# A fused attention and MLP block on one core: reordered weight loads, a spread reciprocal root, a new order in the first block and a split tail

## The chip, the cores and the metric

The kernel runs on one core of a Trainium2 chip. The metric is the device time of one execution in microseconds (us). The span that a profile shows, from the first to the last instruction of the program, is about 2 us shorter (708.9 us where the device time is 710.91). Repeated executions are compared by their median, and ratios are of means.

## The reference, cut to what matters

```python
x = A_x                                             # (1, 2048, 1024), bf16
h  = x + attention(layernorm(x)) @ wo               # 32 heads of 32, window of 256 tokens
h2 = h + silu(layernorm(h) @ w1) @ w2               # w1: 1024 x 3584, w2: 3584 x 1024
```

Tokens are handled in four blocks of 512. The stages follow each other: Q, K and V of block 0; then, for b = 1 to 3, attention of block b-1 woven with the projections of block b; then attention of block 3 woven with the output projections (wo) of blocks 0 to 2; then the MLP of each block. The output projections of block 3 are woven into the first MLP stage.

## The kernel before: the parts that the argument touches

All DMAs are issued from one queue, in program order, on the sync engine (SP in the profile). Attention output is transposed by DMA. The issue of a transpose is deferred to the next step with a list:

```python
late = []
def run_late():
    while late:
        late.pop(0)()
...
def end():                                   # last part of one head group
    attn_out(b, g, 11, 16)
    late.append(lambda: attn_transpose(b, g))
```

The first MLP stage finishes the last head group in its first three iterations (`extra`), then loads four of the seven 1 MB pieces of w2. From iteration 6 on it weaves in the output projections of block 3, which read that last transpose:

```python
run_late()
load_w2(5)
for ft in range(FT):
    acc = h1_group(b, ft)
    run_late()
    if extra:
        extra.pop(0)[0]()
        if not extra and b == 0:
            for i in (1, 2, 3, 4):
                load_w2(i)
    silu(b, acc, ft)
    if b == 0 and 6 <= ft < 14:
        wo_group(NB - 1, *divmod(ft - 6, 2))     # needs every head group's transpose
```

In the attention stages there are only two accumulator banks, and VectorE empties one of them after each group of eight matmuls. VectorE also does the layer normalisation of a coming block, with the reciprocal root by three Newton steps, all in one lump:

```python
def ln_rstd(st, rs, lo, hi):                 # twelve instructions on [128, 4]
    ...
    for _ in range(3):
        nc.vector.scalar_tensor_tensor(out=ta, in0=y, scalar=-0.5, in1=va, ...)
        nc.vector.tensor_tensor(out=ta, in0=ta, in1=y, op=ALU.mult)
        nc.vector.scalar_tensor_tensor(out=y, in0=ta, scalar=1.5, in1=y, ...)
```

The softmax here doesn't subtract the row's maximum and nothing guards it: scores larger than these inputs give would overflow.

## Time and profile before

| | before |
|---|---|
| median of 4 executions, us | 709.91 (707.37 to 710.03) |
| span of the profiled execution, us | 708.9 (device time 710.91, longer than all four above) |
| TensorE busy | 695.2 us, 98% |
| TensorE waits that the profile names | 10.4 us in six entries |

The prediction below shows the main views. In a timeline line, the first two numbers are the start and the length in us, and square brackets give the idle time before it and what ended that. In a window line, the length is followed by the busy time of TensorE, its weight loads, VectorE, ScalarE and GpSimd, then by the granted clock (the share of full speed that TensorE was allowed), the DMA share and GB/s. Two more views help. The first is the page's list of DMA issues (what is written and read, how many, KB each, median us from issue to landing): a transpose of attention output usually lands in 2.5 us, a piece of w2 in 9.0.

```profile
r_a<-in_B_w_dram SPq DMA_DIRECT2D x7, 1024.0 KB, 9.0
...
r_a<-r_n SPq DMA_TRANSPOSE x32, 2.5
```

The second is the page's row of TensorE's granted clock over 40 slices of 17.7 us, in tenths of full speed (9 is 90% or more). One slice, from about 301 to 319 us, shows an 8.

```profile
PEclk9999999999999999989999999999999999999999
```

### The profile page before, as it was taken

To read this page: it belongs to the slowest core of one execution; us is meant where nothing else is said; L and a number is where in the kernel's file an instruction comes from. 1 tells how busy PE (TensorE), PEld (TensorE's weight loads), DVE (VectorE), ACT (ScalarE), POOL (GpSimd) and SP (SyncE) were. 2 spreads that over 40 slices of the span, in tenths; PEclk is the share of its full clock that TensorE was granted. 3 is DMA by queue.
4 is the path that set the end of the run, shared out by engine and by line. 5 is a ranking of instruction groups with operands and counts; after the bars stand their busy time and mean duration, and the time that the engine had idled before them with its cause. 6 is when DMAs were issued, how large, how long until landed. Compare 5 with 4: busy or idle time off the path is not lost.

```text
span 708.9 us, 12138 instructions
## 1 busy us (share of the span) xinstructions
PE 695.2 (98%) x5006; PEld 332.8 (47%) x5006; DVE 288.0 (41%) x606; ACT 259.7 (37%) x335; POOL 172.9 (24%) x375
## 2 busy tenths in 40 slices
PE   8999999999999999979999999999999999999998
PEld 3444555555555554534444444444444444444443
DVE  5347645834443448523332423325134352243111
ACT  3416667777777777511220013300033200233000
POOL 1006566777777777500000000000000000000000
PEclk9999999999999999989999999999999999999999
DMA  9540322125011899780122320021410032200110
GB/s 301 173 120 8 46 54 75 32 55 180 16 23 18 279 265 333 201 276 31 45 69 90 80 75 1 0 67 59 78 35 0 1 97 67 75 1 0 31 38 22
DMA packets 75127, 60.55 MB, mean 85 GB/s; under 512 B 48960, under 2 KB 59200, under 8 KB 75072
## 3 DMA queue, kind: packets, MB, share of 16 engines
q1 hardware_dynamic: 75072, 59.78, 29.9%
q8 instruction: 39, 0.64, 0.4%
q14 instruction: 16, 0.13, 0.1%
HBM read 39.85 MB, written 8.39 MB: 68 GB/s over the span
## 4 chain that ended last, share of the span: by engine, by line
PE 94%; DMA 4%; DVE 2%; SPq 0%; issue 0%
PE hacc L446 18%; PE hacc L483 17%; PE acc L220 16%; PE acc L483 10%; PE acc L446 9%; PE acc L212 8%; PE acc L239 5%; PE o_ps L293 5%; PE sc L257 4%; DMA r_a<-r_n 2%; DMA r_w<-in_A_wqkv_dram 1%; PE hacc L239 1%; DMA r_a<-in_A_x_dram 1%; DVE ln_st L157 0%; DVE r_t L241 0%
## 5 line engine op out<-in xcount | busy, mean ns | idle before, releaser
L268 ACT ACTIVATE r_e<-sc 128x1024 bf16<-128x1024 f32 (+2 forms) x192 | 175.8, 967 | 67.5 <-PE sc L257 54.5
L283 POOL TENSOR_SCALAR_AFFINE_SELECT r_e<-r_e 128x256 bf16<-128x256 bf16 (+1 forms) x368 | 169.9, 490 | 123.1 <-ACT r_e L268 119.7
L446 PEld LDWEIGHTS <-r_w 128*128 128x128 bf16 x896 | 87.8, 98 | 106.1 <-issue 2.4
L483 PEld LDWEIGHTS <-r_a 128*128 128x128 bf16 x896 | 87.7, 98 | 105.7
L483 PE MATMUL hacc<-r_a 128*128 128x512 bf16 x560 | 122.3, 379 | 0.0
L446 PE MATMUL hacc<-r_e,r_w 128*128 128x512 bf16 x456 | 100.9, 379 | 0.0
L455 ACT ACTIVATE r_n<-hacc 128x512 f32<-128x512 f32 x30 | 17.9, 597 | 178.9 <-PE hacc L446 178.9
L483 PE MATMUL acc<-r_a 128*128 128x512 bf16 x336 | 74.0, 379 | 0.0
L220 PEld LDWEIGHTS <-r_w 128*128 128x128 bf16 x512 | 46.1, 98 | 58.6 <-issue 8.9
L222 DVE CAST r_a<-acc 128x512 bf16<-128x512 f32 x56 | 38.6, 690 | 81.0 <-PE acc L220 55.8
L293 PEld LDWEIGHTS <-r_e 128*128 128x128 bf16 x1440 | 50.3, 96 | 22.7
L220 PE MATMUL acc<-r_t,r_w 128*128 128x512 bf16 x256 | 60.8, 380 | 0.0
L220 PE MATMUL acc<-r_w 128*128 128x512 bf16 x256 | 58.2, 380 | 0.0
L293 PE MATMUL o_ps<-r_a,r_e 128*128 128x33 bf16 x1440 | 51.2, 178 | 0.0
L239 PE MATMUL acc<-r_o,r_a 128*128 128x512 bf16 x208 | 49.4, 380 | 1.3 <-DVE r_t L241 1.3
L446 PE MATMUL acc<-r_e,r_w 128*128 128x512 bf16 x216 | 49.1, 379 | 0.0
L239 PEld LDWEIGHTS <-r_a 128*128 128x128 bf16 x256 | 23.3, 98 | 37.2 <-issue 7.4
L257 PE MATMUL sc<-r_a 32*128 32x128 bf16 (+2 forms) x704 | 37.2, 276 | 0.0
L496 DVE SCALAR_TENSOR_TENSOR r_t<-hacc,r_t 128x512 bf16<-128x512 f32 x20 | 13.7, 683 | 56.3 <-PE hacc L483 56.2
L446 PE MATMUL hacc<-r_a,r_w 128*128 128x512 bf16 x144 | 34.6, 393 | 0.0
L496 DVE SCALAR_TENSOR_TENSOR r_t<-acc,r_t 128x512 bf16<-128x512 f32 x12 | 8.3, 692 | 64.2 <-PE acc L483 64.2
L456 DVE SCALAR_TENSOR_TENSOR r_a<-r_n,hacc 128x512 bf16<-128x512 f32 x30 | 20.6, 688 | 33.1 <-ACT r_n L455 33.1
(65 smaller groups left out, 425.4 us busy)
## 6 DMA issues: line engine op xcount, KB each, us to landing
r_w<-in_B_w_dram SPq DMA_DIRECT2D x8, 896.0 KB, 6.8
r_a<-in_B_w_dram SPq DMA_DIRECT2D x7, 1024.0 KB, 9.0
r_w<-in_A_wqkv_dram SPq DMA_DIRECT2D x5, 1024.0 KB, 11.8
r_o<-in_A_x_dram SPq DMA_DIRECT2D x16, 256.0 KB, 5.0
h_dram<-r_t SPq DMA_DIRECT2D x16, 256.0 KB, 2.9
r_t<-h_dram SPq DMA_DIRECT2D x16, 256.0 KB, 2.8
out_dram<-r_t SPq DMA_DIRECT2D x32, 128.0 KB, 1.7
r_e<-h_dram SPq DMA_DIRECT2D x3, 1024.0 KB, 5.8
```

The lines of the kernel that those rows point to most:

```text
L212: nc.tensor.matmul(acc, lhsT=lnT_b[b % 2][:, kt, j * P:(j + 1) * P], rhs=wqkv[:, kt, col0:col0 + 512], start=(kt == 0), stop=(kt == KT - 1))
L220: nc.tensor.matmul(acc, lhsT=wqkv[:, kt, col0:col0 + P], rhs=lnT_b[b % 2][:, kt, :], start=(kt == 0), stop=(kt == KT - 1))
L222: copy(out=(qT, kT)[which][b][:, g, :], in_=acc)
L239: nc.tensor.matmul(acc, lhsT=qT[b][:, g, j * P:(j + 1) * P], rhs=wo[:, g, c * 512:(c + 1) * 512], start=(g == 0), stop=(g == G - 1))
L257: nc.tensor.matmul(sc[hh // 2][:, hh % 2, ch * P:(ch + nq) * P], lhsT=kT[t // 4][r0:r0 + DH, g, (t % 4) * P:(t % 4 + 1) * P], rhs=qT[b][r0 ...
L268: nc.scalar.activation(out=e[:, :, lo:hi], in_=sc[pair][:, :, lo:hi], func=ACT.Exp, scale=scale)
L283: nc.gpsimd.affine_select(out=ap, in_=ap, pattern=[[0, 2], [0, n], [sgn, P]], compare_op=ALU.is_ge if upper else ALU.is_gt, fill=0.0, base ...
L293: nc.tensor.matmul(o_ps[pair][:, qt * 2 + hh, 0:VW], lhsT=e_of(i, kind, pair)[:, hh, ch * P:(ch + 1) * P], rhs=v[:, b * 4 + kt, g * 4 + pa ...
L446: nc.tensor.matmul(acc, lhsT=w1[:, kt, ft * P:(ft + 1) * P], rhs=ln2T[b][:, kt, :], start=(kt == 0), stop=(kt == KT - 1))
L456: nc.vector.scalar_tensor_tensor(out=gT[:, ft, :], in0=th, scalar=1.0, in1=acc, op0=ALU.add, op1=ALU.mult)
L483: nc.tensor.matmul(acc, lhsT=gT[:, ft, j * P:(j + 1) * P], rhs=w2[ft // 4][:, ft % 4, c * 512:(c + 1) * 512], start=(ft == 0), stop=(ft == ...
L496: nc.vector.scalar_tensor_tensor(out=t_out[j % 2][:, c * 512:(c + 1) * 512], in0=acc, scalar=0.5, in1=t_in[j % 2][:, c * 512:(c + 1) * 512 ...
```

## The change

Its intent: take away what TensorE waits for. Separate V weights leave the region of three w1 chunks free earlier; block 0 loads x tiles and weights and orders its V groups in another way, with three warm-up matmuls fewer (matmuls on zeros ahead of the first real work, whose results nobody uses); the Newton steps are spread; four w2 loads come later; the last output columns are split so that the last eviction and store are short. The core of the diff, with cuts marked:

```diff
-    wqkv = view(r_w, 0, KT, 3 * D)
+    wqk = view(r_w, 0, KT, 2 * D)
+    wv = view(r_w, 16384, KT, D)
@@ first loads
     load_x(0, 0)
-    load_wqkv(2 * D, 0, 4)
     load_x(0, 1)
-    load_wqkv(2 * D, 4, 8)
+    load_wqkv(2 * D)
     load_wqkv(2 * D + 512)
@@
-    for i in range(14):
+    for i in range(11):
         nc.tensor.matmul(sc[0][:, i % 2, :], lhsT=warm[:, 0, 0:P], ...)
@@ ln_rstd becomes four steps
+        return [guess, newton, newton, newton]
@@ block 0: V groups (tile, half) around the transposes T1 to T3
-    (0,0) T1 (0,1) (1,0) T2 (1,1) (2,0) T3 (2,1) (3,0) (3,1)
+    (0,0) T1 (1,0) (0,1) T2 (1,1) (2,0) T3 (2,1) (3,0) (3,1)
@@ last projection stage
+                if b == NB - 1 and n in (4, 10, 14):
+                    load_w1({4: 7, 10: 6, 14: 5}[n])
@@ last attention stage
-            if n % 2 == 0 and n // 2 < KT:
-                nc.sync.dma_start(out=w1[:, n // 2, :], ...)
+            if n in (1, 4, 7, 12, 15):
+                load_w1((1, 4, 7, 12, 15).index(n))
@@ first MLP stage
                 extra.pop(0)[0]()
-                if not extra and b == 0:
-                    for i in (1, 2, 3, 4):
-                        load_w2(i)
+            if b == 0 and ft == 3:
+                for i in (1, 2, 3, 4):
+                    load_w2(i)
@@ last second product
+            if b == NB - 1 and j == 3:
+                cols = [(0, 512), (512, 768), (768, 896), (896, 1024)]
```

(The two block 0 lines are shortened to the order in which TensorE gets them. Left out: half of the statistics of x tile 1 is computed earlier in block 0, and two loops take more steps because the Newton steps are now finer.)

## The prediction

> **What bounds the kernel now.** I read the page's table of busy time first, then TensorE's own list of waits, then the windows and the timeline around the longest of those waits.
>
> ```profile
> span 708.9 us, 12138 instructions
> ...
> PE 695.2 (98%) x5006; PEld 332.8 (47%) x5006; DVE 288.0 (41%) x606; ACT 259.7 (37%) x335; POOL 172.9 (24%) x375
> ```
>
> TensorE is busy for 695.2 of 708.9 us. The change removes no matmul of the real work, so what it can win is the remainder, 708.9 - 695.2 = 13.7 us, plus whatever TensorE does at less than full speed. The list of what TensorE waited for says where most of that remainder is:
>
> ```profile
> PE hacc L239 <- DMA r_a<-r_n: 5.3, 1, 5.3
> PE sc L151 <- DVE r_e L146: 1.6, 1, 1.6
> PE acc L212 <- DMA r_w<-in_A_wqkv_dram: 1.5, 2, 1.2
> PE acc L239 <- DVE r_t L241: 1.3, 1, 1.3
> PE acc L212 <- ACT r_w L192: 0.5, 1, 0.5
> PE acc L446 <- issue: 0.2, 1, 0.2
> ```
>
> These six sum to 10.4 us; the other 3.3 us is the end, after the last matmul. Two of them carry the case: 5.3 us in which the first output projection of the last attention block (L239) waits for a DMA transpose, and 1.3 us in which a projection waits for VectorE to empty an accumulator. The timeline shows how the first arises:
>
> ```profile
> 297.98 5.44 SPq L437 DMA_DIRECT2D r_a<-in_B_w_dram  x5
> 303.51 5.97 SPq L313 DMA_TRANSPOSE r_a<-r_n  x1
> 309.22 1.67 PE L239 MATMUL hacc<-r_o,r_a 128*128 128x512 bf16 x7
> 316.20 0.61 PE L239 MATMUL hacc<-r_o,r_a 128*128 128x512 bf16 x1 [5.31 <-DMA r_a<-r_n]
> ```
>
> The sync queue issues five 1 MB loads of w2 and only then the last attention transpose, which lands 12.64 us after its issue in the chain of waits, where the median of that row on the page is 2.5 us. TensorE does the first seven matmuls of the group and stops at 310.9 for the eighth head group. The windows then show a second cost of the same stop:
>
> ```profile
> 310.90:313.90 3.00, 0.00 (x0) 0.00 (x0) 0.00 (x0) 0.00 (x0) 0.00 (x0) 0.99 1.26 355
> 313.90:316.20 2.30, 0.00 (x0) 0.00 (x0) 0.00 (x0) 0.00 (x0) 0.00 (x0) 0.50 0.28 29
> 316.20:320.50 4.30, 4.30 (x11) 1.54 (x12) 0.69 (x1) 0.24 (x1) 0.00 (x0) 0.50 0.00 0
> 320.50:325.00 4.50, 4.50 (x22) 2.06 (x21) 1.74 (x3) 0.96 (x2) 0.00 (x0) 0.98 0.15 58
> ```
>
> The third number from the right is the granted clock. It falls to 0.50 after 3 us of idleness and stays there until 320.5, so the 10 matmuls that start in 316.2 to 320.5 come 0.43 us apart instead of 0.216 us (8 of them take 1.73 us elsewhere in the chain): 10 x (0.427 - 0.216) = 2.1 us. The stop costs 5.3 + 2.1 = 7.4 us in all.
>
> The 1.3 us wait lies behind the twelve small instructions that compute the reciprocal root for the second normalisation in one lump:
>
> ```profile
> 277.81 0.16 DVE L165 TENSOR_SCALAR ln_var<-st_b 128x4 f32<-128x4 f32 x1
> ...
> 280.97 0.56 DVE L169 SCALAR_TENSOR_TENSOR ln_t<-rs_b,ln_var 128x4 f32<-128x4 f32 x1
> 281.56 0.34 DVE L170 TENSOR_TENSOR ln_t<-ln_t,rs_b 128x4 f32<-128x4 f32 x1
> 281.94 0.56 DVE L171 SCALAR_TENSOR_TENSOR rs_b<-ln_t,rs_b 128x4 f32<-128x4 f32 x1
> ...
> 283.15 1.89 PE L239 MATMUL acc<-r_o,r_a 128*128 128x512 bf16 x8 [1.33 <-DVE r_t L241]
> ```
>
> From 277.81 to 282.5 VectorE does nothing else, 4.7 us for work on 4 columns. One attention step of TensorE takes about 2.55 us and there are two accumulators, so the second step after it stands still.
>
> [...] The same L169 instruction takes 161 ns at least and 558 ns at most in its row, the slow ones here beside the masks on GpSimd.
>
> **The change part by part.**
>
> The **w2 loads** 1 to 4 move from the end of the iteration ft = 2 to after the deferred calls of ft = 3. The order of the sync queue in the two kernels confirms what matters: before, five w2 loads and then the transpose; after, one load (w2 5, issued some 5 us earlier), the transpose, and then the other four. VectorE finishes the rows for that transpose at 303.2, it can be issued at about 303.5 as before, and with the usual 2.5 us, even doubled, it lands by 308.5; TensorE needs it at 310.9. The wait goes[...]: -7.4 us. The four loads (4 MB at the 380 GB/s of these windows, 11 us) then land near 315, and their first use is the second MLP product near 367. They stay hidden.
>
> The **Newton steps** become four steps: a guess, and three iterations. In the last attention stage two are done per step of TensorE, so from the durations above the lump of 4.7 us becomes two of about 2.4 and 2.3 us with an accumulator's eviction (0.68) and a normalisation (0.62) between them. Following VectorE instruction by instruction, the eviction of step 17 ends near 280.9 instead of 283.1 and that of step 18 near 284.4, where TensorE wants that accumulator at 284.3: the wait falls from 1.33 to about 0.1. I count -1.2 us. In the three earlier blocks TensorE shows no wait for VectorE, so spreading the steps there wins nothing.
>
> The **w1 chunks**: the separate V weights let three chunks of 896 KB load in the last projection stage (some 190 to 220 us, DMA share 0.2 to 0.3 there), leaving five in the stretch of 240 to 280, where the DMA share is 1.00. TensorE waits for no w1 chunk before, so directly 0. It lightens VectorE's wait for stores (2.9 us before one eviction at 267.4), which only makes the -1.2 safer.
>
> **Block 0**: the first half of the V weights no longer comes ahead of x tile 1. The queue is saturated from 3 to 26 us, and the same bytes lie ahead of x tile 2, which lands at 13.1 (3.3 issued, 9.8 to landing) in both. Its statistics, root and normalisation take 2.7 us, to 15.8, when its transposes run. After, the first V group can only start at about 9.4 (second half landed at 2.27 + 7.1); then the transposes of tile 1, their copies on ScalarE (two of 0.54), and two V groups take TensorE to about 16.0. Five groups and one set of transposes follow in both kernels. Waits of 1.2 + 0.3 + 0.5 become one of about 2 us and one of 0.7, so: 0, give or take 0.4. The three warm-up matmuls are not on the path; data is.
>
> The **tail**: the last 512 columns are split as 256, 128 and 128. [...] transposes of 128 columns in the trace take 0.51/8 = 64 ns[...]. The last eviction shrinks from 0.69 to about 0.3 (estimate: a quarter of the columns, with the 0.16 us that the smallest instruction of VectorE takes as its floor) and the last store from 128 to 32 KB of a 1.7 us landing, -0.2 at most. Net about 0, +-0.3.
>
> **New risks with a price.** With 17 instead of 14 steps, the last two DMA transposes for the first MLP block are issued one attention step later, behind an attention transpose. Before, the last was issued at 292.5, landed 3.2 us later at 295.7, and the MLP started at 295.93 (the 0.2 us of "issue" in the list). After, TensorE arrives at about 294.5; I place the last issue at 291.1 to 293 and the landing at 294.3 to 296.2. Expected cost 0.4 us, at most 1.7. Secondly, after the first transposes TensorE now idles about 2.3 us near 7 to 9.4[...]; I take 0.4.
>
> Sum: 709.9 - 7.4 - 1.2 + 0 + 0 + 0.4 + 0.4 = **702.1 us**.
>
> **The rivals.** (1) The transpose is late for another reason: its issue instruction itself took 5.97 us, and w2 5 is still ahead of it. If half of the delay stayed, the wait would be near 1 us without a clock drop: 703. Against it: w2 5 is issued at 298 and 1 MB needs 3 us. If instead the transposes were late by 7 us or more, 708 or more remains. (2) The freed time is taken back at the MLP's start, by the later transposes: 703.8 at worst. For it speaks that the landing was already within 0.3 us of the start. (3) Everything small goes right too, including the first 10 us: 709.9 - 7.4 - 1.3 - 0.2 - 1.5 gives 699.5. Against it speaks that x tile 2 lands no earlier. (4) [...] the median before might be nearer 708 in another measurement and the gain 6 us, with after unchanged.
>
> **Range and chances.** The end is bounded below by TensorE's work: I see no way under 699. [...] So 699.5 to 705. Faster by 2% would need 695.7, more than all waits that I can name; slower by 2% would need a new stop of 22 us. Hence 1%, 98.5%, 0.5%.
>
> **What would show it.** In the changed profile: the transpose of the last head group issued ahead of four w2 loads and landing in 2.5 to 5 us; no TensorE wait for it; a granted clock of 1.00 through the slices near 310 to 325; no or a tenth of the wait of L239 for VectorE; TensorE's projections of block 1 starting within 0.4 us of 25.6; and a possible new wait of the first MLP group for a transpose. I am wrong if the transpose still lands late, if the clock drops in the first 15 us, or if the MLP's start waits longer than 2 us.

The top of the range was the sum with more for the two risks and for the Newton wait, 705.3. That the clock stays up once the 5.3 us stop is gone, which the -7.4 counts on, was my estimate; the changed profile shows 1.00 from 300 to 325 us. Two figures that belong beside the text, both from the profile before: from 3 to 26 us, where I call the queue saturated, the DMA share was 1.05 at 348 GB/s; and the share I give as 0.2 to 0.3 was 0.21 from 180 to 240 us but 0.09 from 190 to 220.

## The result, and the profile after

| | before | after |
|---|---|---|
| median of 4, us | 709.91 | 701.11 (698.88 to 701.81) |
| span of the profiled execution, us | 708.9 | 700.0 |

The ratio is 0.9879, 95% interval 0.9847 to 0.9911. A ratio is the mean time of one kernel's fast runs over that of the other's of the same rounds, so it is not quite the ratio of the medians quoted. The gain is clear of noise and below 2%.

TensorE's list of waits is down to three entries, all in the first 14 us (columns: who waited, for what, us in total, times, longest):

```profile
PE acc L222 <- DMA r_w<-in_A_wqkv_dram: 2.2, 1, 2.2
PE sc L152 <- DVE r_e L147: 1.6, 1, 1.6
PE acc L222 <- ACT r_w L203: 0.3, 1, 0.3
```

The timeline of the sync queue at the start of the MLP now has one w2 load, the transpose, and then the other four. The trace gives 3.2 us from this transpose's issue to its landing.

```profile
297.64 0.46 SPq L459 DMA_DIRECT2D r_a<-in_B_w_dram  x1
302.46 2.11 SPq L323 DMA_TRANSPOSE r_a<-r_n  x1
304.63 2.62 SPq L459 DMA_DIRECT2D r_a<-in_B_w_dram  x4
308.43 1.89 PE L249 MATMUL hacc<-r_o,r_a 128*128 128x512 bf16 x8
```

All eight matmuls of the projection now run in one piece at 308.43, 2.8 us after the landing at 305.7. The four loads had nobody waiting for them.

To see where the 8.9 us between the two spans lie, I marked in both traces the first weight load of five stages. The table gives the time from each mark to the next.

| stretch | before | after | difference |
|---|---|---|---|
| start to first Q/K weight load | 25.35 | 26.34 | +0.99 |
| to first weight load of an output projection | 207.84 | 207.83 | 0 |
| to first weight load of the MLP (last attention stage) | 62.71 | 60.94 | -1.77 |
| to first weight load of the second product (first MLP stage) | 70.86 | 63.18 | -7.68 |
| to first weight load of the last second product | 290.08 | 290.08 | 0 |
| to the end | 52.06 | 51.63 | -0.43 |
| sum | 708.9 | 700.0 | -8.9 |

The first MLP stage carries the gain. In the last attention stage, the eviction of the critical step comes at 279.91, in time for the group at 282.74 in the timeline, which has no idle time before it:

```profile
279.64 0.34 DVE L178 SCALAR_TENSOR_TENSOR rs_b<-ln_t,rs_b 128x4 f32<-128x4 f32 x1
279.91 0.68 DVE L251 TENSOR_TENSOR r_t<-acc,r_t 128x512 bf16<-128x512 f32 x1
...
282.74 1.90 PE L249 MATMUL acc<-r_o,r_a 128*128 128x512 bf16 x8
```

The start became longer. The windows show a clock drop that the kernel before did not have there:

```profile
10.00:10.86 0.86, 0.86 (x6) 0.35 (x5) 0.00 (x0) 0.00 (x0) 0.00 (x0) 0.92 1.06 373
10.86:12.00 1.14, 1.14 (x7) 0.59 (x6) 0.00 (x0) 0.09 (x1) 0.00 (x0) 0.50 1.08 366
12.00:14.07 2.07, 1.76 (x10) 0.89 (x9) 0.93 (x2) 1.48 (x3) 0.00 (x0) 0.50 1.08 350
14.07:15.00 0.93, 0.93 (x6) 0.39 (x4) 0.56 (x2) 0.29 (x1) 0.00 (x0) 0.96 1.10 350
```

### The profile page after: what moved, and what is told of

Read it like the earlier page. It is cut to its first block, busy times and chain, and to the rows that moved or that the text cites. A ratio compares the mean times of both kernels' runs of the same rounds, so it can differ in the third digit from the quotient of the medians.

```text
span 700.0 us, 12171 instructions
## 1 busy us (share of the span) xinstructions
PE 688.5 (98%) x4970; PEld 336.1 (48%) x5059; DVE 286.3 (41%) x608; ACT 259.7 (37%) x335; POOL 172.2 (25%) x375
## 4 chain that ended last, share of the span: by engine, by line
PE 97%; DMA 1%; issue 1%; ACT 0%; SPq 0%; DVE 0%
PE hacc L468 18%; PE hacc L505 17%; PE acc L230 16%; PE acc L505 10%; PE acc L468 9%; PE acc L222 8%; PE acc L249 7%; PE o_ps L303 5%; PE sc L267 4%; PE hacc L249 1%; DMA r_w<-in_A_wqkv_dram 1%; PE o_ps L202 0%; SPq L127 0%; ACT r_a L224 0%; ACT r_w L203 0%
## 5 line engine op out<-in xcount | busy, mean ns | idle before, releaser
L505 PEld LDWEIGHTS <-r_a 128*128 128x128 bf16 x952 | 90.9, 98 | 103.0
L505 PE MATMUL hacc<-r_a 128*128 128x512 bf16 (+2 forms) x605 | 121.9, 359 | 0.6
L230 PE MATMUL acc<-r_w 128*128 128x512 bf16 x246 | 57.7, 380 | 0.5
L249 PEld LDWEIGHTS <-r_a 128*128 128x128 bf16 x256 | 23.1, 98 | 29.6 <-issue 5.1
L520 DVE SCALAR_TENSOR_TENSOR r_t<-hacc,r_t 128x512 bf16<-128x512 f32 (+2 forms) x22 | 14.0, 635 | 56.6 <-PE hacc L505 56.6
L222 PE MATMUL acc<-r_w 128*128 128x512 bf16 x122 | 30.4, 390 | 2.8 <-DMA r_w<-in_A_wqkv_dram 2.2
```

The costliest lines, as they stand in the source:

```text
L222: nc.tensor.matmul(acc, lhsT=lnT_b[b % 2][:, kt, j * P:(j + 1) * P], rhs=wv[:, kt, c * 512:(c + 1) * 512], start=(kt == 0), stop=(kt == KT ...
L230: nc.tensor.matmul(acc, lhsT=wqk[:, kt, col0:col0 + P], rhs=lnT_b[b % 2][:, kt, :], start=(kt == 0), stop=(kt == KT - 1))
L249: nc.tensor.matmul(acc, lhsT=qT[b][:, g, j * P:(j + 1) * P], rhs=wo[:, g, c * 512:(c + 1) * 512], start=(g == 0), stop=(g == G - 1))
L505: nc.tensor.matmul(acc[:, 0:c1 - c0], lhsT=gT[:, ft, j * P:(j + 1) * P], rhs=w2[ft // 4][:, ft % 4, c0:c1], start=(ft == 0), stop=(ft == F ...
L520: nc.vector.scalar_tensor_tensor(out=t_out[j % 2][:, c0:c1], in0=acc[:, 0:c1 - c0], scalar=0.5, in1=t_in[j % 2][:, c0:c1], op0=ALU.mult, o ...
```

## The experiments

Twelve runs were made, all correct; run 5 repeats the changed kernel and run 10 repeats run 4. Runs 1 to 4 shared one chip (kernel before: median 708.97), runs 5 to 8 a second (708.70), runs 9 to 12 a third (708.79). My theory: the late transpose, with the half clock that follows it, is the gain; the other parts matter by a microsecond at most. The rivals: another part of the change carries a good share, or the transpose is slow for reasons other than its place in the queue.

### 1. Only the w2 loads

```diff
 # the kernel before
                 extra.pop(0)[0]()
-                if not extra and b == 0:
-                    for i in (1, 2, 3, 4):
-                        load_w2(i)
+            if b == 0 and ft == 3:
+                for i in (1, 2, 3, 4):
+                    load_w2(i)
```

> The kernel before with one edit: w2 loads 1 to 4 are issued after the deferred calls of ft = 3. Theory (the last attention transpose stood behind the loads in the sync queue, and the stop of TensorE also halved its clock): the transpose lands 2.5 to 4 us after issue, the 5.3 us wait and the half clock near 314 to 320 vanish, and the stretch from the first MLP weight load to the first second-product weight load shrinks from 70.9 to about 63.2 us; total 7 to 8 us less, near 702.3. Rival (the transpose is slow of itself or waits for the one load that stays ahead): it lands 6 us or more after issue and less than 4 us is won. Second rival (most of the gain of the change comes from its other parts): under 5 us is won here.

Measured: median 700.76, ratio 0.9894 (0.9871 to 0.9916). The transpose landed 2.4 us after issue, the wait was gone, and the stretch was 360.2 - 297.0 = 63.2 us. One loop moved does nearly all that the whole change does; both rivals fall.

The profiled run was the slowest of its four, 704.33 against 700.35 to 700.96, for a reason that belongs to another part. VectorE came late in the last attention stage and TensorE stood for 1.73 us; the windows show that the clock then fell, and the group after the stop took 3.52 us instead of 1.90.

```profile
282.99 3.52 PE L239 MATMUL acc<-r_o,r_a 128*128 128x512 bf16 x8 [1.73 <-DVE r_t L241]
```
```profile
282.00:284.00 2.00, 1.01 (x3) 0.40 (x3) 1.93 (x6) 1.32 (x2) 1.42 (x4) 0.77 0.14 54
284.00:286.00 2.00, 2.00 (x6) 0.73 (x5) 1.69 (x4) 0.00 (x0) 0.36 (x1) 0.50 0.60 163
```

### 2. Only the Newton steps

```diff
 # the kernel before
-        steps.append(lambda: ln_rstd(st, rs, 0, 4))
+        steps += rstd_steps(st, rs)          # in both normalisations
@@
-            for _ in range(1 if n < 17 else 2):
+            for _ in range(1 if n < 16 else 2):
@@ second products
-                for _ in range(2):
+                for _ in range(3):
```

> The kernel before with only the Newton iteration cut into four steps, with the step counts that the change uses. Theory: the last attention stage, from its first output projection to the first MLP weight load, shrinks from 62.7 to about 61.0 us because the 1.3 us wait for VectorE goes; nothing else moves; total 1.3 to 1.8 us less, near 708.2. Rival (the change's fewer w1 loads in that stage were needed for it): the wait stays at 0.5 us or more and the stage stays above 61.8 us.

Measured: median 708.98, ratio 0.9997 (0.9984 to 1.0010). The stage is 292.8 - 231.7 = 61.1 us as expected and the wait is gone, but the time is not 1.3 us less. The expectation was a miss in the total. Why shows when the stage is read in every profile:

| Newton steps | last attention stage, us, one profile each |
|---|---|
| in one lump (before, runs 1, 3, 12) | 62.7, 64.8, 61.0, 62.8 |
| spread (after, runs 2, 4 to 11) | 60.9, 61.1, 61.2, 61.0, 60.9, 61.1, 61.1, 61.2, 61.0, 61.0 |

With the lump the wait is there in some executions and not in others: run 3 has the lump and no wait at all. With the spread the stage is steady in all ten profiles. Run 2 lies between 708.00 and 709.30, the kernel before in the same set between 707.91 and 710.70; six executions are few to call the slow ones gone. That it moves the median is not shown; the interval allows a gain of at most 0.16%, 1.1 us.

### 3. Filling the stop with idle work

```diff
 # the kernel before, in wo_group
         for g in range(G):
+            if (b, j, c, g) == (NB - 1, 0, 0, G - 1):
+                for _ in range(22):
+                    nc.tensor.matmul(o_ps[0] as one bank, lhsT=w1[:, 0, 0:P], rhs=w1[:, 0, 0:512],
+                                     start=True, stop=True)      # result thrown away
             nc.tensor.matmul(acc, lhsT=qT[b][:, g, ...], rhs=wo[:, g, ...], ...)
```

> The kernel before with 22 matmuls on data that is already there, results thrown away, put before the eighth matmul of the projection that waits for the late transpose. They take 22 x 0.216 = 4.75 us of the 5.3 us stop. Theory (the stop costs 5.3 us of waiting and 2.1 to 2.3 us of half clock after it): the transpose still lands at about 316, TensorE waits about 0.5 us, the clock stays at full, and the total falls by 2.1 to 2.3 us, near 707.6. Rival (the half clock is not caused by the idleness or costs nothing on the path): no change, 709.9.

Measured: median 706.73 against 708.97, ratio 0.9968 (0.9949 to 0.9986). All four executions list a mean clock of 1.000, where all eleven executions of the kernel before in this set list 0.995. The list of waits and the window around the landing:

```profile
PE hacc L243 <- DMA r_a<-r_n: 0.4, 1, 0.4
```
```profile
312.00:315.00 3.00, 2.56 (x12) 1.00 (x11) 0.69 (x1) 0.00 (x0) 0.00 (x0) 1.00 0.01 1
```

The transpose is as late as before and the work is 22 matmuls more, yet the kernel is 2.2 us faster. So this stop costs its length and, separately, 2.2 us of half clock after it.

### 4. The old block 0 in the changed kernel

```diff
 # the changed kernel
-    load_x(0, 0); load_x(0, 1); load_wqkv(2 * D)
+    load_x(0, 0); load_wqkv(2 * D, 0, 4); load_x(0, 1); load_wqkv(2 * D, 4, 8)
-    for i in range(11):
+    for i in range(14):
-    (0,0) T1 (1,0) (0,1) T2 (1,1) (2,0) T3 (2,1) (3,0) (3,1)
+    (0,0) T1 (0,1) (1,0) T2 (1,1) (2,0) T3 (2,1) (3,0) (3,1)
```

> The changed kernel with the load order, the order of V groups and the 14 warm-up matmuls of the kernel before in block 0; everything else as changed. Theory (in the profiled run the new order of block 0 costs 1.0 us, because the first V group waits until 9.5 us for its whole weights and the short idle time drops the clock once): the first Q/K weight load comes at 25.3 to 25.4 us instead of 26.3, and the total falls by 0.5 to 1.0 us against the changed kernel, near 700.2. Rival[...]: the median is within 0.3 us of the changed kernel's, 701.1.

Measured: median 699.66 (699.33 to 699.78), ratio 0.9868 (0.9850 to 0.9885), clock 1.000 in all runs, first Q/K weight load at 23.6, so both fell by more than expected. The start differs between executions or chips (the same kernel has 25.0 in run 10), so the comparison with the changed kernel needed its own set; runs 5 to 12 are about that.

### 5. The changed kernel again

> The changed kernel again, unedited, as the yardstick of this set. Expected 699.9 to 701.8. If the clock drop of the profiled run (0.50 from 10.9 to 14.1 us) belongs to the idle time ahead of the first V group, some of the runs list a mean clock of 0.997 to 0.998 and are about 1 us longer than those at 1.000; if the two do not go together, the drop is not what makes them longer.

Measured: median 700.65, ratio 0.9885 (0.9868 to 0.9902). Four runs at clock 1.000 take 699.80 to 700.71; the one at 0.995 takes 702.98. The same holds for the first four runs of the changed kernel: 698.88 and 700.66 at 1.000, 701.55 at 0.997 and 701.81 at 0.998. The clock drop and the longer time go together, by 1.9 us in the mean of the first four runs and 2.7 here rather than the 1 us that I expected.

### 6. Filler matmuls ahead of the first V group

```diff
 # the changed kernel
+    for i in range(5):
+        nc.tensor.matmul(sc[0][:, i % 2, :], lhsT=warm[:, 0, 0:P], rhs=warm[:, 0, :], start=True, stop=True)
     v_group(0, 0, 0, act)
```

> The changed kernel with five matmuls on zeros, results thrown away, between the first transposes and the first V group, where TensorE waits 2.2 us for weights; they take 1.1 us at full clock and 2.1 at half. Theory (the start of the changed kernel loses to the clock and not to the order of the groups): every run lists 1.000, no run is over 0.5 us above the fastest, and the median falls by 0.3 to 1.0 us against the changed kernel of this set. Rival (the order itself is slower because the first V group waits for all of its weights): no gain over 0.2 us.

Measured: median 700.50 (700.01 to 701.60), ratio 0.9882. No run dropped the clock, but the median fell by only 0.15 us and the runs spread over 1.6 us: by its own numbers a miss for the theory, which had counted on most runs of the yardstick dropping, and only one did; the rival's number, no gain over 0.2 us, was met. In the profile of this run the weights landed later than in run 5 (first V group at 10.31 instead of 9.37); the landing of the first loads differs from one execution to the next by up to a microsecond and hides what is left.

### 7. The tail in one piece

```diff
 # the changed kernel
-                cols = [(0, 512), (512, 768), (768, 896), (896, 1024)]
+                cols = [(0, 512), (512, 1024)]
```

> The changed kernel with the last 512 columns in one piece as before. By the profiles (52.06 us before, 51.63 after, from the first weight load of the last second product to the end) the split wins 0.4 us, so this should be 0.4 us slower than the changed kernel of this set, with that stretch at 52.0 to 52.1 us. Rival (my forecast: net 0): the stretch is within 0.1 us of 51.63.

Measured: the stretch is 701.5 - 649.4 = 52.1 us, as in the kernel before; with the split it was 51.6 in the changed kernel and in its repetition. So the split wins 0.4 to 0.5 us, and my forecast of net 0 was off. The total, 703.21 median, says nothing about the tail: five of the six runs list a clock below 1.000 (702.56 to 704.39), and the one that does not took 700.32. In the profiled run, one of the five, the clock is at 0.50 from 9.2 to 12.6 us; where it fell in the others is not recorded.

### 8. Another order in block 0: x tile 2 ahead

```diff
 # run 4's kernel
-    load_wqkv(2 * D + 512)
     load_x(0, 2)
+    load_wqkv(2 * D + 512)
     load_x(0, 3)
-    (0,0) T1 (0,1) (1,0) T2 (1,1) (2,0) T3 (2,1) (3,0) (3,1)
+    (0,0) T1 (1,0) T2 (0,1) (2,0) (1,1) T3 (2,1) (3,0) (3,1)
```

> Everything of the change except block 0, which goes another way: V weights of the first 512 columns in two halves around x tile 1, then x tile 2, and only then the V weights of the second 512 columns; the V groups follow in the order in which their data land. Theory (the end of block 0's projections of V is set by the landing of x tile 2, followed by 2.7 us of normalisation): the first Q/K weight load comes 0.5 to 1 us earlier than with the old order of block 0 (23.6 to 25.3 us in the runs so far), and the total is 0.5 to 1.5 us below the changed kernel, near 699.0. Rival (TensorE's own work from its first V group on is the bound, or the clock drops in a new gap): within 0.3 us of the old order, 699.7.

Measured: median 699.60 (699.03 to 700.14), ratio 0.9870 (0.9854 to 0.9886), clock 1.000 in all four. The first Q/K weight load comes at 23.3 us, the earliest of all profiles. It is 1.05 us below the changed kernel's median on the same chip, and two of its four runs are below the fastest of it, though the intervals of the two ratios overlap.

### 9. Only the old order of loads

```diff
 # the changed kernel; its V groups and its 11 warm-up matmuls stay
-    load_x(0, 0); load_x(0, 1); load_wqkv(2 * D)
+    load_x(0, 0); load_wqkv(2 * D, 0, 4); load_x(0, 1); load_wqkv(2 * D, 4, 8)
```

> The changed kernel with only the order of the first loads of before (half of the first V weights, x tile 1, the other half); its new order of V groups and its 11 warm-up matmuls stay. Theory (block 0 of the changed kernel loses because its first V group waits for all of its weights, and x tile 2 lands later behind the new order: 13.0 to 14.0 us in four profiles, 11.3 to 13.1 in five of the old order): the first V group starts by 8.2 us, the first Q/K weight load comes by 24.6, no clock drop, and the total is near 699.7, 0.5 to 1 us below the changed kernel. Rival (the new order of V groups is what costs): total stays near 700.6.

Measured: median 701.95, ratio 0.9899 (0.9881 to 0.9917). Three of five runs dropped the clock (701.95, 702.56, 703.13); the other two took 699.87. The profiled run, one of the two, does have its first V group at 8.13 and its first Q/K weight load at 24.1. So the theory is right about the profile and wrong about the time: in the profiled run the wait for weights is gone, and three others still list a lower clock. Where it fell in them is not recorded. What this kernel shares with the changed one and not with run 10 is the number of warm-up matmuls and the order of the V groups and their normalisation.

### 10. The old block 0, again

The kernel of run 4, unedited.

> The kernel of the earlier run with the old block 0 in the changed kernel, again, unedited, as the yardstick of this set and as the candidate for the fastest: 699.3 to 700.3, clock 1.000 in every run. If it comes out at 700.6 or more, its lead over the changed kernel was that of another chip.

Measured: median 700.47 (699.77 to 700.51), clock 1.000 in all runs. Its profile had x tile 2 at 12.7 us, against 11.3 in run 4, and the first Q/K weight load at 25.0: this is no faster than what the changed kernel takes in runs that do not drop the clock. Part of run 4's lead was the chip, or the execution.

### 11. All w1 loads late

```diff
 # the changed kernel
-                if b == NB - 1 and n in (4, 10, 14): load_w1(...)
-            if n in (1, 4, 7, 12, 15): load_w1(...)
+            if n % 2 == 0 and n // 2 < KT: load_w1(n // 2)
```

> The changed kernel with all eight w1 loads in the last attention stage as before. Theory (the earlier w1 loads win nothing by themselves, since TensorE waits for no w1 chunk, and the Newton steps alone hold the stage at 61.0 us): total within 0.4 us of the changed kernel, 700.7, and the stage from the first output projection to the first MLP weight load at 60.9 to 61.2 us. Rival (the lighter DMA queue is what keeps VectorE in time): the stage grows to 61.8 us or more and TensorE waits for VectorE there.

Measured: median 700.73, against 700.65 of the changed kernel on another chip; the stage is 293.3 - 232.3 = 61.0 us and TensorE does not wait for VectorE. The early w1 loads win nothing measurable, as the theory says.

### 12. Two of four loads ahead

```diff
 # the kernel before
                 if not extra and b == 0:
-                    for i in (1, 2, 3, 4):
+                    for i in (1, 2):
                         load_w2(i)
+            elif b == 0 and ft == 3:
+                for i in (3, 4):
+                    load_w2(i)
```

> The kernel before with two of the four w2 loads left ahead of the last attention transpose and two moved behind it. Theory (the transpose lands when what stands ahead of it in the queue has been moved; 4 MB more of it made the landing 12.6 us, against 2.4 with none): 2 MB at 380 GB/s less is 5.5 us less, so it lands 6.5 to 7.5 us after issue, and the wait of TensorE is 0 to 0.5 us; total near 702. Rival (any load ahead blocks it, or a fixed delay of the transpose): 10 us or more, and a wait of over 2 us.

Measured: 700.74 and 701.96, ratio 0.9897 (0.9879 to 0.9915). The timeline of the sync queue has three loads (the one for w2 5 among them), the transpose, and two loads:

```profile
296.62 1.62 SPq L437 DMA_DIRECT2D r_a<-in_B_w_dram  x3
301.97 1.19 SPq L313 DMA_TRANSPOSE r_a<-r_n  x1
303.21 2.21 SPq L437 DMA_DIRECT2D r_a<-in_B_w_dram  x2
```
```profile
DMA to landing us min/median/max: 7.3/7.3/7.3
```

With five loads ahead of it the transpose landed after 12.6 us, with three after 7.3: (12.6 - 7.3)/2 = 2.65 us for each 1 MB load. In run 12 no matmul waits for it any more. The 2.4 us of run 1 is not a third point on this line: there the one load ahead, issued at 299.46, landed 5.3 us later, at 304.8, and the transpose was issued only at 304.33, so hardly anything was left ahead of it. In the other two profiles the last load ahead landed at 315.8 and 308.8, and the transpose 0.4 to 0.5 us after it. What delays it is the loads ahead that have not landed when it is issued; the "any load blocks it" and "fixed delay" rivals fall.

## Why the prediction was right, point by point

The prediction was 702.1 in 699.5 to 705; 701.11 was measured. By its steps:

- **w2 loads, -7.4 us.** Right in mechanism and nearly in size: the stretch lost 7.68 us. Run 1 shows that this part alone does it, run 12 that the place in the queue sets the landing, and run 3 that the half clock is a cost of its own: 2.2 us measured against 2.1 worked out.
- **Newton steps, -1.2 us.** Right in the profile (the wait was 1.33 and is 0, the stage is 1.77 shorter), wrong as a term of the median. The step that failed is reading one execution's wait as a property of the kernel: in run 3 it is absent with the lump in place, and run 2 finds no gain in the median. In the profile of before, an eviction of that stage had waited 2.9 us for a store; run 1 shows 4.2 us there and the longest stop. In run 12 it is 3.0 us, and TensorE stops for 1.3; in run 3 it is 2.3 us, for a load of x, and TensorE does not wait for VectorE. So a late transfer seems to set whether the lump hurts. That last link is argued from the profiles, not tested.
- **w1 chunks, 0.** Right (run 11).
- **Block 0, 0 +-0.4, and 0.4 for the stop ahead of the first V group.** Right without a drop, as far as runs on different chips can say: the changed kernel at full clock (699.80 to 700.71, run 5) and the old block 0 (699.77 to 700.51, run 10) take the same. Mis-sized was the risk. A clock below 1.000 was listed in 13 of the 25 runs of kernels with 11 warm-up matmuls and no filler (changed kernel 2 of 4, runs 5, 7, 9 and 11: 1 of 5, 5 of 6, 3 of 5, 2 of 5), and it cost 1.9 to 3.1 us in the mean of each kernel. In kernels with 14 warm-ups and no long stop later (runs 1, 3, 4, 8, 10, 12) it was 2 of 22, both in run 1, one of them the VectorE stop shown there; with the filler 0 of 4. So the term is about 13/25 x 2.5 = 1.3 us, not 0.4. This price of the stop ahead of the first V group is the step that failed, and two of the prediction's own signs came out against it: the clock dropped in the first 15 us, and the projections of block 1 began at 26.3, not within 0.4 us of 25.6. My sentence that the three warm-up matmuls "are not on the path" is in doubt. Whether it is their number or the order of the V groups that brings the drops was not separated: runs 9 and 10 differ in both.
- **The tail, 0 +-0.3.** Slightly off. The matmuls of the three pieces take 6.20 us in the chain of waits against 6.06 in one piece: +0.14. The evictions of the two pieces of 128 columns start 1.56 us apart, at 695.71 and 697.27: 56 ns for each of 28 matmuls, so the 64 ns of a transpose did not apply. The last eviction went from 0.69 to 0.29 us: -0.40. From its end to the end of the span it is 2.44 instead of 2.61 us: -0.17. The sum is -0.43, as measured.
- **The later transposes at the start of the MLP, +0.4 expected.** They did not show: the last was issued at 291.7 us and the MLP began at 295.1 without a wait. That is 0.4 us less than counted.

The traces also suggest why only some executions drop the clock. A trace's clock record begins when the clock first becomes full, at 4.5 to 7.3 us; from there matmuls come 0.22 instead of 0.43 us apart. Each drop in the traces comes a whole number of windows of 3.41 us after that moment: at 7.31 + 3.41 us in the changed kernel, at 5.81 + 3.41 in run 7, 81 windows later in run 1 and 90 in the kernel before (from 6.67 to 313.87 us, 307.20 us at full clock, or 90 x 3.413). These are such windows of the changed kernel, of run 1 and of run 5:

```profile
7.31:10.73 3.42, 1.25 (x6) 0.68 (x7) 0.90 (x3) 0.85 (x3) 0.00 (x0) 1.00 1.08 361
279.66:283.08 3.42, 1.69 (x29) 1.02 (x27) 3.15 (x10) 2.83 (x4) 2.60 (x6) 1.00 0.68 255
4.49:7.90 3.41, 1.76 (x13) 0.84 (x12) 2.81 (x8) 1.46 (x4) 0.00 (x0) 1.00 0.94 286
```

After the first two, in which TensorE was busy for 1.25 and 1.69 us, the clock fell. After the third, with 1.76 us, it stayed full, and so it did after the next one of run 5, with 1.95 us, though a stop of 2.35 us lies across the two. In all traces the fullest window at full clock that was followed by a drop has 1.69 us and the emptiest that was not has 1.76. So in these traces the fall of the clock goes with the busy time of such a window, at most 1.69 us before a fall and at least 1.76 us without one, and the moment at which the windows begin decides how a stop is divided between them. (Busy times are the profile's, whose matmul ends are modelled, and this was read afterwards from one profile of each run; no run tested it.)

So the total was right partly by errors that cancel: the MLP's start cost 0.4 less and the tail 0.4 less than I counted, and the clock at the start took about 0.9 more. The base was favourable too: 709.91 in this set of four against 708.70 to 708.97 in the three later sets, a difference as large as the Newton term that run 2 does not find in the median; on the second chip the change wins 8.05 us and not 8.8. One sum has a slip without consequence: the second rival's 703.8 counts 0.4 us twice, and 702.1 + 1.3 is 703.4. The lowest median is run 8, 699.60 against 700.65 for the changed kernel and 708.70 for the kernel before on one chip; its lead over the changed kernel is not clear of noise.

## What to carry to other kernels

In this kernel's queue a small transfer that someone waited for also waited for the bytes still ahead of it, 2.65 us for each 1 MB. Issue such a transfer before bulk loads whose use is far away; moving one loop can be worth more than many refinements. When TensorE is 98% busy, look at the granted clock beside each wait, since a stop can be paid twice (5.3 us of waiting and 2.2 us of half clock here). Before a wait seen in one profile becomes a term in a sum, look for it in a second execution.
